# The end of the last down unit taken apart by product, and the second token tile back on the common load queue

## The chip, the cores and the metric

The kernel runs on one core of a Trainium2 chip. The metric is device microseconds of one execution. The times below are from four runs of the kernel before; one of them was profiled.

The engines are named as in the profile: PE (TensorE, matrix products; PEld its weight loads), DVE (VectorE), ACT (ScalarE), POOL (GpSimd), and SP, which here only issues DMA transfers. PE writes its products into PSUM, which has eight banks of 512 float32 columns per partition; DVE and ACT bring them from there to SBUF.

## The reference, cut to what matters

x is (1, 2048, 1024), all weights are bfloat16.

```python
xn = layernorm(x)
# linear attention, 32 heads of 32
q, k, v = split(xn @ wqkv)
pq, pk = phi(q), phi(k)                    # phi(t) = where(t > 0, t + 1, exp(t)) + 1e-6
kv = einsum("bhsd,bhse->bhde", pk, v); z = einsum("bhsd->bhd", pk)
s = (pq @ kv / (pq @ z + 1e-6)) @ wo
# feed-forward, F = 3584
g = silu((silu(xn @ w_gate) * (xn @ w_up)) @ w_down)
return x + s * g
```

## The kernel before, in words

The work is in stages that run one behind the other on PE.

**QKV stage** (to about 130 us). x is cut into 16 tiles of 128 tokens (`NT`), the K and V weights into four chunks of 512 columns (`NCH`, tile `wkv_sb`). Each token tile i is loaded (`load_x`), its statistics are taken by DVE (`emit_stats`, L409 and L410), the inverse deviation is made (for tiles 0 and 1 by ACT's square root, L422; from tile 2 by a Newton iteration, `emit_rstd`, on DVE for tile 2 and on POOL from tile 3), and it is normalised by DVE (`emit_N`, L447). PE needs it transposed. For tiles 0 to 3 (`NPE` = 4) PE transposes it itself (`emit_TR`, L474), and ACT or DVE copies the result out of PSUM (L479, L477); from tile 4 a transposing DMA on SP's queue does (L464). Then come four products per tile, `emit_Bmm(i, c)` (L490), eight matmuls each into one of three PSUM banks `kv_ps`. `emit_Bev(i, c)` empties a bank: for K by ACT (L144 and L151) and DVE (L152 and L153), for V by an ACT copy (L505). `emit_C(i)` (L512) accumulates K times V over all tiles.

The order on PE, DVE, ACT and POOL is that of the calls, written out by hand for the first tiles (a `manual_schedule`); each engine runs its instructions in that order and waits where its operands or its buffer are not ready. SP's queue is in the order of the calls too. The loads of x, of the K and V weights and then of the Q and output weights (12 MB in all) stand on it one behind the other, and the transposing DMAs of tiles 4 and up stand behind them. In the kernel before, three transfers go another way or have a special place: half of tile 0 and all of tile 1 are issued by ACT (L354, L357), and tile 1 is treated in halves like tile 0. PE's order in the first part is: products (0,0); transposes of 1; (0,1), (1,0), (1,1), (0,2); transposes of 2; (1,2), (2,0), (0,3), (1,3); C(0); transposes of 3; C(1); (2,1) and on.

**Attention stage** (to about 230 us), then **the feed-forward** in two passes of 1024 tokens. Its gate and up products (L731) and its down product (L916) are done by a scheme with seven products of half-size blocks in place of eight, whose sums are put together on DVE.

**The down product** (`emit_down`). A unit t (four per pass) is 128 tokens in each half of a pass, and has four output blocks of 128 by 512. Phase "a" makes one of them, and partial sums that three others need; for units 0 and 1 these are kept in SBUF (`kept`: s1 for one block, s34 for two). Phase "b" then adds three more products of 14 matmuls each (`prods_b`): two go to the two halves of a two-bank tile `dzw`, one to a bank `dx`. For units 0 and 1 the products are fresh in PSUM and DVE adds the kept partials on evacuation (`evac_b`, L975 and L976), ACT applies Silu with a scale (L977, L978), and `fin` multiplies by s and adds x on DVE (L888, L889) and stores the block (L890, on SP's queue in the last pass).

The very last unit, t = 1 of the last pass, is made by `finish`. PE runs the two products of `dzw` one after the other, then that of `dx`. DVE adds the kept partials to both halves of `dzw` in one instruction of 1024 columns (L1000), ACT applies Silu to both in one (L1001), and both blocks go through `fin`. For `dx`, DVE adds the kept partial in two instructions of 256 columns (L1008), each followed by ACT's Silu (L1009), and `fin` runs on each half of 256 columns with a store of its own.

The PSUM pools of this stage are `pps` (four tiles of one bank, tag "s") and `ppd` (two tiles of two banks, tag "d").

Of the kernel before, what the change touches and what calls it, by code (L numbers as in the profile page):

```python
# [9 lines left out]
ACT = mybir.ActivationFunctionType  # L10
ALU = mybir.AluOpType
FP32 = mybir.dt.float32
BF16 = mybir.dt.bfloat16
I32 = mybir.dt.int32
F32R = mybir.dt.float32r
F16 = mybir.dt.float16
# [5 lines left out]
def kernel(  # L22
# [11 lines left out]
    nc = tc.nc  # L34
    P = 128
    x2 = A_x.flatten_outer_dims()
# [295 lines left out]
    with ExitStack() as p1:  # L332
# [12 lines left out]
        def x_ap(i):  # L345
            return xp_tiles[i // 4][:, i % 4, :]
# [3 lines left out]
        def load_x(i):  # L350
            if i == 0 and D % 2 == 0:
                h = D // 2
                x_loads[i] = nc.sync.dma_start(out=x_ap(i)[:, 0:h], in_=x2[0:P, 0:h])
                nc.scalar.dma_start(out=x_ap(i)[:, h:D], in_=x2[0:P, h:D])  # L354
                return
            if i == 1:
                x_loads[i] = nc.scalar.dma_start(out=x_ap(i), in_=x2[i * P:(i + 1) * P, :])  # L357
                return
            x_loads[i] = nc.sync.dma_start(out=x_ap(i), in_=x2[i * P:(i + 1) * P, :])

        def load_wkv(c, halves=1):
            hs = DC // halves
            return [nc.sync.dma_start(out=wkv_sb[:, h * hs:(h + 1) * hs, c * CW:(c + 1) * CW],
                                      in_=wqkv_v[:, h * hs:(h + 1) * hs, D + c * CW: D + (c + 1) * CW])
                    for h in range(halves)]
# [1 line left out]
        NCH = 2 * NCC  # L367
        first_wave = min(2 * TPB, NT)
        load_x(0)
        load_x(1)  # L370
        load_wkv(0, halves=2 if DC % 2 == 0 else 1)
        nx = 2
        for c in range(1, NCH):
            load_wkv(c)
            if nx < NT:
                load_x(nx)
                nx += 1
        for i in range(nx, NT):
            load_x(i)
        for wt, wv in ((wq_sb, wqkv_v), (wo_sb, wo_v)):  # L380
# [71 lines left out]
        def emit_N(i):  # L452
            xn = xnw.tile([P, D], BF16, name="xn", tag="xn")
            xn_tiles[i] = xn
            if i < 2:
                for hh in range(2):
                    cols = slice(hh * (D // 2), (hh + 1) * (D // 2))
                    emit_norm(i, xn[:, cols], cols=cols)
            else:
                emit_norm(i, xn[:])  # L460
            ln_state.pop(i)
            if i >= NPE:
                xn_tiles.pop(i)
                nc.sync.dma_start_transpose(out=xn_ap(slice(0, DC), slice(i * P, (i + 1) * P)), in_=xn[:])  # L464

        def emit_TR(i):
            tok = slice(i * P, (i + 1) * P)
            xn = xn_tiles.pop(i)
            nh = 2 if i < 2 else 1
            dch = DC // nh  # L470
            for hh in range(nh):
                tr_ps = psC.tile([P, dch, P], BF16, name="tr_ps", tag="C")
                for dc in range(dch):
                    nc.tensor.transpose(tr_ps[:, dc, :], xn[:, (hh * dch + dc) * P:(hh * dch + dc + 1) * P], ident[:])  # L474
                dst = xn_ap(slice(hh * dch, (hh + 1) * dch), tok)
                if i == 1 and hh == 0:
                    nc.vector.tensor_copy(out=dst, in_=tr_ps[:])  # L477
                else:
                    nc.scalar.copy(out=dst, in_=tr_ps[:])  # L479
# [5 lines left out]
        def emit_Bmm(i, c):  # L485
            tok = slice(i * P, (i + 1) * P)
            kv_ps = psB.tile([P, CW], FP32, name="kv_ps", tag="B")
            kv_banks[(i, c)] = kv_ps
            for dc in range(DC):
                mm = nc.tensor.matmul(kv_ps[:], lhsT=xn_ap(dc, tok), rhs=wkv_sb[:, dc, c * CW:(c + 1) * CW],  # L490
                                      start=(dc == 0), stop=(dc == DC - 1))
                if dc == 0 and c == 0:
                    marks[("B", i)] = mm
# [49 lines left out]
        emit_Bev(1, 0)  # L543
        emit_Bmm(1, 1)
        emit_Bmm(0, 2)
        emit_TR(2)
        emit_Bev(1, 1)
        emit_Bev(0, 2)
        emit_Bmm(1, 2)
        emit_Bev(1, 2)  # L550
        emit_N(3)
        ln_pre(4)
        emit_Bmm(2, 0)
        emit_Bmm(0, 3)
        emit_Bev(0, 3)
        emit_Bmm(1, 3)
# [1 line left out]
        emit_C(0)  # L558
        for i in range(2, NT):
            for c in range(NCH):  # L560
                if (i, c) != (2, 0):
                    emit_Bmm(i, c)
                if c == 0:
                    if i + 1 < NPE:
                        emit_TR(i + 1)
                    emit_C(i - 1)
                emit_Bev(i, c)
                if c == 3 and i in (4, 6, 7):
                    prep(1)
                if i >= 8 and c % 2 == 1:  # L570
                    k = 2 * (i - 8) + c // 2
                    prep(11 * (k + 1) // 16 - 11 * k // 16)
                if c % 2 == 1:
                    for k in (PRE_AT[i - 1] if i - 1 in PRE_AT else (4,) if i == 2 else ())[c // 2:c // 2 + 1]:
                        emit_N(k)
                    for k in PRE_AT.get(i, ())[c // 2:c // 2 + 1]:
                        ln_pre(k)
# [140 lines left out]
    with ExitStack() as p3:  # L718
# [7 lines left out]
        def k2(shape, dt, name):  # L726
            return kp.tile(shape, dt, name=name, tag="k2")
# [156 lines left out]
        def fin(p, t, cc, y, eng1, eng2, out_eng, cols=None):  # L884
            io = io_tiles[(p, t, cc)]
            r0 = p * TB2 + t * P
            cs = cols or slice(0, CW)
            eng1.tensor_tensor(out=y[:, cs], in0=y[:, cs], in1=io[:, 1, cs], op=ALU.mult)  # L888
            eng2.tensor_tensor(out=io[:, 0, cs], in0=y[:, cs], in1=io[:, 0, cs], op=ALU.add)  # L889
            out_eng.dma_start(out=out2[r0:r0 + P, cc * CW + cs.start:cc * CW + cs.stop], in_=io[:, 0, cs])  # L890
            if cs.stop == CW:
                io_load()

        def emit_down(p, h, base, last, more_S, next_S):
# [5 lines left out]
            def wb(k, q):  # L900
                t = w_tiles[(p, "b", k // 2)]
                v = t[:].rearrange("p h a b -> p (h a b)")[:, 0:6 * CW].rearrange(
                    "p (k q n) -> p k q n", k=2, q=3)[:, k % 2, q]
                return v.bitcast(F16) if q == 2 else v
# [4 lines left out]
            def alloc(t, phase):  # L909
                x_ = pps.tile([P, CW], FP32, name="dx", tag="s")  # L910
                y_ = pps.tile([P, CW], FP32, name="dy", tag="s") if phase == "a" else None
                zw = ppd.tile([P, 2, CW], FP32, name="dzw", tag="d")
                bk[t] = (x_, y_, zw)

            def mm(out, lhs, rhs, first, lastk):
                nc.tensor.matmul(out, lhsT=lhs, rhs=rhs, start=first, stop=lastk, skip_group_check=True)  # L916
# [12 lines left out]
            def prods_b(t, k, fresh):  # L929
                x_, y_, zw = bk[t]  # L930
                f, l = fresh and k == 0, k == NFG - 1
                t2 = slice(TB + t * P, TB + (t + 1) * P)
                return [lambda: mm(x_[:], h[:, 2 * k + 1, t * P:(t + 1) * P], wb(k, 0), f, l),
                        lambda: mm(zw[:, 0, :], h[:, 2 * k + 1, t2], wb(k, 2), f, l),
                        lambda: mm(zw[:, 1, :], h[:, 2 * k, t2].bitcast(F16), wb(k, 1), f, l)]
# [51 lines left out]
                        lambda: fin(p, t, 0, g11, *fin_e)]  # L987

            def finish(t):
                alloc(t, "b")  # L990
                x_, _, zw = bk[t]
                s1, s34 = kept[t]
                for q in (1, 2):
                    for k in range(NFG):
                        prods_b(t, k, True)[q]()
                d = m4.tile([P, 2, CW], FP32, name="dd", tag="m4")
                c11 = k2([P, CW], FP32, "c11")[:]
                g_ = k2([P, 2, CW], BF16, "g12")
                g11 = k2([P, CW], BF16, "g11")[:]
                nc.vector.tensor_tensor(out=d[:], in0=zw[:], in1=s34, op=ALU.add)  # L1000
                nc.scalar.activation(out=g_[:], in_=d[:], func=ACT.Silu, scale=rch)  # L1001
                fin(p, t + TPB, 0, g_[:, 0, :], *fin_e)
                fin(p, t, 1, g_[:, 1, :], *fin_e)
                for k in range(NFG):
                    prods_b(t, k, True)[0]()
                hs_ = [slice(i * CW // 2, (i + 1) * CW // 2) for i in range(2)]
                for cs in hs_:
                    nc.vector.tensor_tensor(out=c11[:, cs], in0=x_[:, cs], in1=s1[:, cs], op=ALU.add)  # L1008
                    nc.scalar.activation(out=g11[:, cs], in_=c11[:, cs], func=ACT.Silu, scale=rch)  # L1009
                for cs in hs_:  # L1010
                    fin(p, t, 0, g11, *fin_e, cols=cs)

            NS = NFG + LEAD
# [209 lines left out]
```

## Time and profile before

| | us |
|---|---|
| median of 4 runs | 766.25 |
| the four runs | 765.86, 765.88, 766.63, 767.33 |
| the profiled run | 765.88 |
| its span | 764.0 |
| outside the span | 1.88 |
| mean granted TensorE clock | 0.999 |

The span is the time from the first to the last event of the core's profile; the time of a run has 1.88 us more in it. Rows of the timeline read: start, duration (both us from the span's start), engine, line of the kernel, operation, output tile and input tiles, shapes, count; in brackets the idle time of that engine just before, and what ended it. A group of several matmuls is shown as one row; a single 512-column matmul is listed with 379 ns, but they overlap, and start 216 ns apart (14 of them stretch over 3.19 us, that is 13 x 0.216 + 0.379). "PEq", "SPq" and the like are the sequencers that issue.

### The profile page before, as it was taken

To read this page: it belongs to the slowest core of one execution; us is meant where nothing else is said; L and a number is where in the kernel's file an instruction comes from. 1 tells how busy PE (TensorE), PEld (TensorE's weight loads), DVE (VectorE), ACT (ScalarE), POOL (GpSimd) and SP (SyncE) were. 2 spreads that over 40 slices of the span, in tenths; PEclk is the share of its full clock that TensorE was granted. 3 is DMA by queue.
4 is the path that set the end of the run, shared out by engine and by line. 5 is a ranking of instruction groups with operands and counts; after the bars stand their busy time and mean duration, and the time that the engine had idled before them with its cause. 6 is when DMAs were issued, how large, how long until landed. Compare 5 with 4: busy or idle time off the path is not lost.

```text
span 764.0 us, 10416 instructions
## 1 busy us (share of the span) xinstructions
PE 748.6 (98%) x3648; PEld 349.2 (46%) x3717; DVE 551.1 (72%) x1075; ACT 347.2 (45%) x476; POOL 287.7 (38%) x413
## 2 busy tenths in 40 slices
PE   8999999999999999999999999999999999999996
PEld 3444444444444444444444444444444444444443
DVE  7788567997666688888889875368676776787335
ACT  4535666788953566566448311132322223201111
POOL 0577599959674256868655000100000000200000
PEclk9999999999999999999999999999999999999999
DMA  9956867669789669898888136498644455520923
GB/s 316 350 102 122 213 247 250 268 214 279 229 292 272 247 233 314 299 345 299 298 301 301 65 104 246 126 379 313 231 171 166 166 173 180 189 105 28 296 70 118
DMA packets 105396, 170.29 MB, mean 223 GB/s; under 512 B 34688, under 2 KB 82176, under 8 KB 94720
## 3 DMA queue, kind: packets, MB, share of 16 engines
q1 hardware_dynamic: 94816, 120.74, 50.3%
q0 software_dynamic: 7936, 44.31, 14.8%
q10 hardware_dynamic: 2592, 4.59, 1.8%
q8 instruction: 29, 0.48, 0.2%
q14 instruction: 23, 0.19, 0.1%
HBM read 111.67 MB, written 50.59 MB: 212 GB/s over the span
## 4 chain that ended last, share of the span: by engine, by line
PE 88%; DVE 6%; DMA 2%; issue 1%; POOL 1%; ACT 1%; SPq 0%; DVEq 0%; ACTq 0%
PE zw L731 25%; PE xb L731 12%; PE dzw L916 12%; PE kv_ps L490 11%; PE s_ps L665 7%; PE yb L731 6%; PE dx L916 6%; PE q_ps L170 4%; PE dy L916 3%; DMA xp<-in_A_x_dram 1%; DMA xnT<-xn 1%; PE kvz L512 1%; DVE o_blk L646 1%; PE nd_ps L638 1%; DVE pqT L141 1%
## 5 line engine op out<-in xcount | busy, mean ns | idle before, releaser
L731 PEld LDWEIGHTS <-w_sb 128*128 128x128 f16 (+1 forms) x1568 | 152.2, 98 | 182.8
L490 PE MATMUL kv_ps<-wkv_sb,xnT 128*128 128x512 bf16 x499 | 113.0, 379 | 3.1 <-DMA wkv_sb<-in_A_wqkv_dram 0.9
L731 PE MATMUL xb<-xnT,w_sb 128*128 128x512 bf16 x420 | 113.3, 379 | 1.5
L731 PE MATMUL zw<-S,w_sb 128*128 128x512 f16 x448 | 105.8, 379 | 0.0
L731 PE MATMUL zw<-xnT,w_sb 128*128 128x512 bf16 x448 | 105.8, 379 | 0.0
L280 POOL TENSOR_TENSOR w_sb<-w_sb 128x512 f16<-128x512 bf16 x42 | 48.9, 1165 | 95.6 <-DVE w_sb L268 36.3
L247 ACT ACTIVATE w_sb<-w_sb 128x2048 bf16<-128x2048 bf16 x42 | 79.9, 1902 | 6.1 <-DMA w_sb<-in_B_w_up_dram 5.3
L916 PE MATMUL dx<-w_sb,hT 128*128 128x512 bf16 x216 | 79.7, 379 | 0.3
L490 PEld LDWEIGHTS <-xnT 128*128 128x128 bf16 x512 | 48.6, 97 | 58.6 <-issue 1.6
L916 PEld LDWEIGHTS <-hT 128*128 128x128 bf16 (+1 forms) x448 | 43.8, 98 | 52.8
L916 PE MATMUL dzw<-w_sb,hT 128*128 128x512 bf16 (+1 forms) x217 | 63.0, 379 | 0.1
L170 PE MATMUL q_ps<-xnT,wq_sb 128*128 128x512 bf16 x249 | 57.9, 379 | 0.4
L665 PE MATMUL s_ps<-wo_sb,oT 128*128 128x512 bf16 x250 | 57.4, 379 | 0.3
L731 PE MATMUL yb<-S,w_sb 128*128 128x512 f16 x224 | 57.4, 378 | 0.0
L759 DVE SCALAR_TENSOR_TENSOR s<-yb,rc_all,s 128x512 f32<-128x512 f32 x42 | 31.5, 749 | 35.4 <-ACT s L758 35.2
L807 ACT ACTIVATE sg<-cg 128x1024 bf16<-128x1024 f32 x28 | 29.6, 1057 | 57.6 <-DVE cg L800 57.5
L800 DVE SCALAR_TENSOR_TENSOR cg<-zw,rc_all,s 128x1024 f32<-128x1024 f32 x28 | 35.9, 1283 | 25.4 <-PE zw L731 14.0
L856 POOL TENSOR_TENSOR hs<-hT 128x512 f16<-128x512 bf16 x2 | 2.5, 1254 | 132.6 <-ACT sg L807 132.6
L281 POOL TENSOR_TENSOR w_sb<-w_sb 128x512 f16<-128x512 bf16 x42 | 50.1, 1193 | 3.3
L283 POOL TENSOR_TENSOR w_sb<-w_sb 128x512 f16<-128x512 bf16 x42 | 50.8, 1210 | 0.0
L282 POOL TENSOR_TENSOR w_sb<-w_sb 128x512 f16<-128x512 bf16 x42 | 49.8, 1186 | 0.0
L890 POOL DMA_DIRECT2D out_dram<-io x16 | 8.7, 542 | 101.9 <-DVE io L889 101.6
(148 smaller groups left out, 1100.9 us busy)
## 6 DMA issues: line engine op xcount, KB each, us to landing
w_sb<-pk_g SPq DMA_DIRECT2D x27, 1024.0 KB, 5.7
pk_g<-w_sb POOLq DMA_DIRECT2D x14, 1024.0 KB, 5.1
pk_u<-w_sb POOLq DMA_DIRECT2D x14, 1024.0 KB, 5.8
w_sb<-wd SPq DMA_DIRECT2D x14, 1024.0 KB, 5.2
w_sb<-pk_u SPq DMA_DIRECT2D x14, 1024.0 KB, 5.0
w_sb<-wd SPq DMA_DIRECT2D x14, 768.0 KB, 4.5
w_sb<-in_B_w_gate_dram SPq DMA_DIRECT2D x14, 512.0 KB, 4.9
w_sb<-in_B_w_down_dram SPq DMA_DIRECT2D x28, 256.0 KB, 3.4
```

The costliest lines, as they stand in the source:

```text
L170: nc.tensor.matmul(q_ps[:], lhsT=wq_sb[:, dc, g * P:(g + 1) * P], rhs=xn_ap(dc, btok), start=(dc == 0), stop=(dc == DC - 1))
L247: nc.scalar.activation(out=junk, in_=raw_view(key, t), func=ACT.Square, accum_out=asum[:])
L280: nc.gpsimd.tensor_tensor(out=T1, in0=b12, in1=b11, op=ALU.subtract)
L281: nc.gpsimd.tensor_tensor(out=T2, in0=b22, in1=T1, op=ALU.subtract)
L282: nc.gpsimd.tensor_tensor(out=T3, in0=b22, in1=b12, op=ALU.subtract)
L283: nc.gpsimd.tensor_tensor(out=T4, in0=b21, in1=T2, op=ALU.subtract)
L490: mm = nc.tensor.matmul(kv_ps[:], lhsT=xn_ap(dc, tok), rhs=wkv_sb[:, dc, c * CW:(c + 1) * CW], start=(dc == 0), stop=(dc == DC - 1))
L665: mm = nc.tensor.matmul(s_ps[:], lhsT=oT[:, c, ttok], rhs=wo_sb[:, c, cc * CW:(cc + 1) * CW], start=(c == 0), stop=(c == G - 1))
L731: mm = nc.tensor.matmul(out, lhsT=lhs(k), rhs=rhs(k), start=(first and k == 0), stop=(k == HK - 1), skip_group_check=True)
L759: nc.vector.scalar_tensor_tensor(out=s2[:], in0=y_[:], scalar=rc, in1=s1[:], op0=ALU.mult, op1=ALU.add)
L800: nc.vector.scalar_tensor_tensor(out=d12, in0=zw[:], scalar=rc, in1=s2[:, None, :].to_broadcast([P, 2, TB]), op0=ALU.mult, op1=ALU.add)
L916: nc.tensor.matmul(out, lhsT=lhs, rhs=rhs, start=first, stop=lastk, skip_group_check=True)
```

## The change

Two places are changed.

In the QKV stage, tile 1 is no longer issued on ACT's queue: it goes on SP's queue, after the two halves of the first weight chunk and ahead of the second chunk. It is normalised in one instruction and transposed in one group of eight, and DVE in place of ACT copies the transposes of tiles 0 and 1 out of PSUM. The transposes of tile 2 and its first product (2,0) move back: PE's order becomes (0,0); transposes of 1; (0,1), (1,0), (1,1), (0,2), (1,2); transposes of 2; (0,3), (1,3); C(0); (2,0); transposes of 3; C(1); (2,1) and on.

In `finish`, each product gets a PSUM bank of its own: product 0 half of a two-bank tile (`dz`), product 1 a bank `df0`, and the last product two banks `df1` and `df2`, 256 columns in each. Products 0 and 1 each have their own addition and Silu of 512 columns. The kept partial of the last block is copied by ACT into `df1` and `df2` ahead of the products, and PE accumulates on it (`first` is False for all matmuls of that product), so that no addition follows. The last product runs in two column halves one after the other, 14 matmuls of 256 columns each, with its weights loaded for each half; Silu reads each half from PSUM.

```diff
@@ load_x @@
-            if i == 1:
-                x_loads[i] = nc.scalar.dma_start(out=x_ap(i), in_=x2[i * P:(i + 1) * P, :])
-                return
             x_loads[i] = nc.sync.dma_start(out=x_ap(i), in_=x2[i * P:(i + 1) * P, :])
...
         load_x(0)
-        load_x(1)
         load_wkv(0, halves=2 if DC % 2 == 0 else 1)
-        nx = 2
+        nx = 1
         for c in range(1, NCH):
-            load_wkv(c)
             if nx < NT:
                 load_x(nx)
                 nx += 1
+            load_wkv(c)
@@ emit_N @@
-            if i < 2:
+            if i == 0:
@@ emit_TR @@
-            nh = 2 if i < 2 else 1
+            nh = 2 if i == 0 else 1
...
-                if i == 1 and hh == 0:
+                if i < 2:
                     nc.vector.tensor_copy(out=dst, in_=tr_ps[:])
                 else:
                     nc.scalar.copy(out=dst, in_=tr_ps[:])
@@ order of the first tiles @@
         emit_Bmm(0, 2)
-        emit_TR(2)
         emit_Bev(1, 1)
...
         ln_pre(4)
-        emit_Bmm(2, 0)
+        emit_TR(2)
         emit_Bmm(0, 3)
...
         for i in range(2, NT):
             for c in range(NCH):
-                if (i, c) != (2, 0):
-                    emit_Bmm(i, c)
+                emit_Bmm(i, c)
@@ finish(t) @@
-                alloc(t, "b")
-                x_, _, zw = bk[t]
+                ps = [ppd.tile([P, 2, CW], FP32, name="dz", tag="d")[:, 0, :]]
+                ps += [pps.tile([P, CW], FP32, name="df%d" % i, tag="s")[:] for i in range(3)]
                 s1, s34 = kept[t]
-                for q in (1, 2):
+                t1, t2 = slice(t * P, (t + 1) * P), slice(TB + t * P, TB + (t + 1) * P)
+                hs_ = [slice(i * CW // 2, (i + 1) * CW // 2) for i in range(2)]
+                for i in range(2):
+                    nc.scalar.copy(out=ps[2 + i][:, 0:CW // 2], in_=s1[:, hs_[i]])
+                for q, (r0, cc) in enumerate(((t + TPB, 0), (t, 1))):
                     for k in range(NFG):
-                        prods_b(t, k, True)[q]()
-                d = m4.tile([P, 2, CW], FP32, name="dd", tag="m4")
-                c11 = k2([P, CW], FP32, "c11")[:]
-                g_ = k2([P, 2, CW], BF16, "g12")
+                        lhs = h[:, 2 * k, t2].bitcast(F16) if q else h[:, 2 * k + 1, t2]
+                        mm(ps[q], lhs, wb(k, 2 - q), k == 0, k == NFG - 1)
+                    d = k2([P, CW], FP32, "d%d" % q)[:]
+                    g_ = k2([P, CW], BF16, "g%d" % q)[:]
+                    nc.vector.tensor_tensor(out=d, in0=ps[q], in1=s34[:, q, :], op=ALU.add)
+                    nc.scalar.activation(out=g_, in_=d, func=ACT.Silu, scale=rch)
+                    if q == 0:
+                        f0 = (r0, cc, g_)
+                fin(p, *f0, *fin_e)
+                fin(p, r0, cc, g_, *fin_e)
                 g11 = k2([P, CW], BF16, "g11")[:]
-                nc.vector.tensor_tensor(out=d[:], in0=zw[:], in1=s34, op=ALU.add)
-                nc.scalar.activation(out=g_[:], in_=d[:], func=ACT.Silu, scale=rch)
-                fin(p, t + TPB, 0, g_[:, 0, :], *fin_e)
-                fin(p, t, 1, g_[:, 1, :], *fin_e)
-                for k in range(NFG):
-                    prods_b(t, k, True)[0]()
-                hs_ = [slice(i * CW // 2, (i + 1) * CW // 2) for i in range(2)]
-                for cs in hs_:
-                    nc.vector.tensor_tensor(out=c11[:, cs], in0=x_[:, cs], in1=s1[:, cs], op=ALU.add)
-                    nc.scalar.activation(out=g11[:, cs], in_=c11[:, cs], func=ACT.Silu, scale=rch)
-                for cs in hs_:
+                for i, cs in enumerate(hs_):
+                    o_ = ps[2 + i][:, 0:CW // 2]
+                    for k in range(NFG):
+                        mm(o_, h[:, 2 * k + 1, t1], wb(k, 0)[:, cs], False, k == NFG - 1)
+                    nc.scalar.activation(out=g11[:, cs], in_=o_, func=ACT.Silu, scale=rch)
                     fin(p, t, 0, g11, *fin_e, cols=cs)
```

## The prediction, on record before the changed kernel ran

> **What bounds the kernel now.** I read the page first, then the chain of work that ended last, then the timeline of the two places that the change touches: the first 45 us and the last 16 us.
>
> ```profile
> span 764.0 us, 10416 instructions
> PE 748.6 (98%) x3648; PEld 349.2 (46%) x3717; DVE 551.1 (72%) x1075; ACT 347.2 (45%) x476; POOL 287.7 (38%) x413
> PE 88%; DVE 6%; DMA 2%; issue 1%; POOL 1%; ACT 1%; SPq 0%; DVEq 0%; ACTq 0%
> ```
>
> TensorE (PE) is busy 98% and carries 88% of the chain. So the change can move the time only where PE waits or where the span runs on after PE's last matmul. Such places are few: the start, and the tail behind PE's last product.
>
> The run that was profiled took 765.88 us for its span of 764.0, so 1.88 us lie around the span. The median of the four runs is 766.25, 0.37 above that run. I work out a difference in the span and take it from the median.
>
> **The tail, before.** This is the timeline of the last 10 us: start, duration, engine, line, operation, and what ended the idle time.
>
> ```profile
> 754.88 3.19 PE L916 MATMUL dx<-w_sb,hT 128*128 128x512 bf16 x14
> 755.08 1.23 DVE L1000 TENSOR_TENSOR dd<-dzw,kept 128x1024 f32<-128x1024 f32 x1 [1.05 <-PE dzw L916]
> 756.34 1.15 ACT L1001 ACTIVATE g<-dd,hsc 128x1024 bf16<-128x1024 f32 x1 [4.29 <-DVE dd L1000]
> 757.52 0.43 DVE L888 TENSOR_TENSOR g<-g,io 128x512 bf16<-128x512 bf16 x1 [1.21 <-ACT g L1001]
> ...
> 758.78 0.42 DVE L889 TENSOR_TENSOR io<-g,io 128x512 bf16<-128x512 bf16 x1
> 759.12 0.75 DVE L1008 TENSOR_TENSOR c<-dx,kept 128x256 f32<-128x256 f32 x2
> 759.57 0.91 ACT L1009 ACTIVATE g<-c,hsc 128x256 bf16<-128x256 f32 x2 [2.08 <-DVE c L1008]
> 760.12 0.29 DVE L888 TENSOR_TENSOR g<-g,io 128x256 bf16<-128x256 bf16 x1 [0.24 <-ACT g L1009]
> ...
> 760.97 0.29 DVE L889 TENSOR_TENSOR io<-g,io 128x256 bf16<-128x256 bf16 x1
> ```
>
> PE ends at 758.07 (754.88 + 3.19), but VectorE (DVE) only takes up PE's last result at 759.12: it is still busy with the two products before, whose joint 1024-wide addition could not start until both were done (755.08). Its last addition ends at 761.26, 3.19 us after PE. What follows (the last store's issue, landing, the end) takes 2.74 us to 764.0 and is not touched.
>
> **The tail, after.** Product 0 now ends by itself, 14 matmuls earlier. The 28 matmuls before 755.05 are spaced 0.216, so product 0 is done at 755.05 - 14 x 0.216 = 752.03. DVE is then still writing out the unit before (its last L889, at 753.60 for 0.42, ends 754.02). The 512-wide addition takes 0.68 (L976, same shapes): 754.05 to 754.73. The Silu takes 0.70 (L978): to 755.46. Product 1 is done at 755.05: addition 755.08 to 755.76, Silu 755.79 to 756.49. Four multiplications and additions of L888 and L889 stretch over 1.60 (757.52 to 759.12 above) and start at 755.79: they end at 757.40, while PE is still at work.
>
> The last product becomes 28 matmuls of 256 columns, with 14 more weight loads. No row has 256 columns. The nearest are 512 columns, spaced 0.216, and 129 columns with a fresh weight load each (L512), eight in 0.46 on the chain, so 0.058 each. In a straight line between them 256 columns cost 0.110. So 28 take 3.05 instead of 14 x 0.216 = 3.02, and PE ends near 758.10. Bounds: no less than half of 0.216 (3.02 in all), no more than a full 0.216 each (6.05, +3.0 us). I take 0.110: the 129-column row shows pairs of load and matmul at half that spacing, so the load is hidden.
>
> A weight load reads 97 to 98 ns as busy on the page. The Trainium skill ("TensorE: Matmul & The Clock Gate", the section on LDWEIGHTS) gives columns / 1.2 ns for it, 107 ns for 128 columns; if loads could overlap nothing, 14 more would cost an estimated 1.5 us by that page and the time would be 765.8. The L512 row, a load and a matmul every 0.058, speaks against that.
>
> The kept partial no longer has to be added by DVE after PE: two ScalarE (ACT) copies of 256 columns put it into the banks ahead. The 512-wide copy L955 takes 0.585, so each takes at most that. They stand on ACT behind L978, free at 752.05, and are done by 753.2; PE's first matmul of the last product waits for them and comes at 754.88: cover of 1.6 us. Behind them on ACT stands product 0's Silu, not ready before 754.73. Copying into the accumulator bank appears in no row; twice the time would still be covered.
>
> The end is then a short chain. PE's second half ends at 758.10; Silu from PSUM, 256 wide, 0.50 (L1009; L983 and L978 take 0.69 and 0.70 from PSUM and from SBUF, so the source does not matter): 758.13 to 758.63. Then L888 and L889 as at 760.65 to 761.26, 0.61: 758.68 to 759.29. The first half is done by 758.0 beside PE. **Gain: 761.26 - 759.29 = 1.97 us.** SP's store queue has no work between 758.4 and 759.3, so the last store goes at once.
>
> **The start.** Token tile 1 loses its own queue (ACT) and goes on SP behind both halves of the first weight chunk; its normalisation loses its halves; DVE instead of ACT evacuates the transposes of tiles 0 and 1; tile 2's transposes and its first product go back to later places. These are rows of the timeline:
>
> ```profile
> 8.89 0.65 PE L474 MATMUL tr_ps<-ident,xn 128*128 128x128 bf16 x8
> ...
> 10.43 7.07 PE L490 MATMUL kv_ps<-wkv_sb,xnT 128*128 128x512 bf16 x31 [0.89 <-DMA wkv_sb<-in_A_wqkv_dram]
> ...
> 11.10 1.29 DVE L409 BATCH_NORM_STATS2 stats<-xp 128x6 f32<-128x512 bf16 x2 [1.36 <-DMA xp<-in_A_x_dram]
> ```
>
> Before, tile 1 landed at 1.20 + 4.4 = 5.6. The later half of the weight chunk landed near 7.4 (issued at 1.67; the two halves took 5.2 in the median, the faster 4.7, so the slower 5.7). Behind it tile 1 lands near 7.4, since the sum of bytes is the same. Statistics of tile 1 start at 7.45, not 6.26 (DVE's two new copies, 0.42 each, end at 7.34). Normalisation starts 2.09 later as before, 9.54, takes 0.54 in one piece, and the eight transposes start at 10.18 and let PE go on at 10.65. Before, PE went on at 10.43 because of the second weight chunk, whose place in the bytes is unchanged: +0.22.
>
> DVE then copies tile 1's transposes (two times 0.42), so tile 2's statistics start at 11.67, not 11.10: the DVE chain is 0.57 late, and with it ScalarE's L144 and L151 for the product (1,0), ended by L153 at 16.56, now 17.13. They free its bank at 18.34. Product (1,2) takes that bank, and PE is ready for it at 10.65 + 32 x 0.216 = 17.56, since tile 2's transposes no longer stand ahead of it. PE idles 0.8. The old wait of 0.32 at 20.03 and the 0.17 that the transposes took longer there go. Added up, PE reaches the product (2,1), where the orders agree again, at 27.1 instead of 26.57: **0.55 late**.
>
> That lateness meets a wait. First the chain, then the timeline:
>
> ```profile
> 31.73 0.55 DVE xn L447
> 32.30 7.81 DMA xnT<-xn
> 40.16 1.25 PE kv_ps L490 x5
> ```
>
> ```profile
> 40.16 1.90 PE L490 MATMUL kv_ps<-wkv_sb,xnT 128*128 128x512 bf16 x7 [0.88 <-DMA xnT<-xn]
> ```
>
> PE waits 0.88 for tile 4's transposing DMA. That was issued at 32.30, yet the DMA view shows the engines full (about 350 GB/s) to past 37, on the weight loads ahead of it in the same queue; later transposes land in 3.1. So the landing at 40.1 is set by the end of the loads, and issuing it 0.57 later changes nothing (some 4 us of slack). PE arrives at 39.28 + 0.55 = 39.83, still too early. **The start costs 0.** If that cover goes, it costs what is left over: lateness minus 0.88. Below nothing: at most 0.3 is to be had, if the loads drain sooner. Above: see B and D.
>
> **Sum.** 764.0 - 1.97 = 762.0 for the span, 763.9 for a run like the profiled one; 766.25 - 1.97 = **764.3** for the median, 0.26% less. What a measurement of this kernel can tell from no change is about 0.2%, 1.53 us, so faster means below 764.7 and slower above 767.8.
>
> **Rivals.**
>
> A, the forecast (0.61): 763.4 to 764.8 with the scatter of the runs.
>
> B, the start outlasts its cover (0.17): between the first product's end (7.0 + 8 x 0.216 = 8.7) and 10.18 PE now idles 1.5 us, where it idled 0.89. The warm-up matmuls of 512 columns (eleven at 0.43 in 1.49 to 5.88) show that PE starts at half rate. If the longer idle time brought that back for as long, the loss is some 3.6 / 2 = 1.8: 0.55 + 1.8 - 0.88 = 1.5, giving 765.8. A DVE or ACT chain 0.6 later than I reckon gives 764.6 to 765. Against it: 0.89 idle at 9.54 left the next 32 matmuls at 0.216.
>
> By the Trainium skill (the same page, "The HAM clock gate") the clock falls only after an idle window of about 3.4 us, which would make the first of these nothing; no row here has such a gap after the warm-up.
>
> C, weight loads show in the 256-column matmuls (0.12 in all): each 0.01 us above 0.110 costs 0.27. At 0.14 to 0.18 the time is 765.1 to 766.2 (0.08). The gain is gone at 0.110 + 1.97 / 27 = 0.183, and beyond it the kernel is **slower**: at the bound of 0.216 the end is 3.0 later, 764.3 + 3.0 = 767.3 (0.04, of which 0.03 by over 0.2% only with B added). Against: the L512 row.
>
> D, the transposing DMA lands elsewhere (0.10): 256 KB move from one DMA queue to another, 0.73 us at 350 GB/s; either sign. Earlier: 764.0. Later: up to 765.0.
>
> That the change does not do what it says would be a Silu on the first half that waits for the second; the halves have separate banks and each Silu its own wait on PE, so I give this nothing of its own.
>
> **Chances.** Faster by over 0.2%: A 0.60, and 0.05 of D and 0.01 of B: 0.66. Slower by over 0.2%: 0.03, from C with B. Within: 0.31. Range: from 763.4 (A with D's gain) to 766.0 (B and most of C), leaving out C's far end.
>
> **What would show it.** Tail: the last DVE row ends 1.2 us behind PE's last matmul instead of 3.2; 28 matmuls of 256 columns in about 3.2; no DVE addition behind PE. Start: PE waits once near 17.6 to 18.4 for ACT, comes to the wait at 40.1 with 0.3 left of 0.88, and all is level from there to 748. The prediction is wrong if PE's last product begins later than 754.9, or if its spacing exceeds 0.12.

## The result, and the profile after

Over 40 runs the changed kernel takes 765.31 us in the median (763.63 to 767.86), the kernel before, over 61 runs, 766.58 (lowest 765.6). The ratio is **0.9979 (95% interval 0.9970 to 0.9987)**: 0.21% faster, where 0.26% was forecast. Ratios here compare undisturbed runs alone, so they are not quite the quotients of the medians.

The run that was profiled took 767.84 us, the second slowest of all, and its span is longer than that of before, though the kernel is faster. So this profile is to be read place by place, not as a whole. Its page:

```profile
span 766.1 us, 10444 instructions
...
PE 92%; DVE 4%; ACT 1%; issue 1%; DMA 1%; SPq 0%; ACTq 0%; DVEq 0%
```

PE's share of the chain (the work that ended last, followed back) is 92% instead of 88: PE carries the start as well now, behind tile 1's load (2.21 to 8.92 in the chain), and DVE has less of the tail.

The tail, from the timeline of the last 13 us (a group's row shows the shape of its first matmul only; 28 of these are 256 wide):

```profile
755.89 6.24 PE L910 MATMUL df<-w_sb,hT 128*128 128x512 bf16 x41
...
756.00 0.66 ACT L990 COPY df<-kept 128x256 f32<-128x256 f32 x2
...
759.17 0.68 DVE L997 TENSOR_TENSOR d<-df,kept 128x512 f32<-128x512 f32 x1
...
760.64 0.47 ACT L1008 ACTIVATE g<-df,hsc 128x256 bf16<-128x256 f32 x1
...
762.17 0.47 ACT L1008 ACTIVATE g<-df,hsc 128x256 bf16<-128x256 f32 x1 [1.05 <-PE df L910]
762.68 0.29 DVE L882 TENSOR_TENSOR g<-g,io 128x256 bf16<-128x256 bf16 x1 [0.37 <-ACT g L1008]
763.00 0.29 DVE L883 TENSOR_TENSOR io<-g,io 128x256 bf16<-128x256 bf16 x1
```

PE ends at 762.13 and DVE's last row at 763.29, 1.16 us behind it; before it was 3.19. The end gained 2.03 us, and no DVE addition stands behind PE.

The start, from the timeline of the first 48 us:

```profile
8.94 1.29 DVE L405 BATCH_NORM_STATS2 stats<-xp 128x6 f32<-128x512 bf16 x2 [1.65 <-DMA xp<-in_A_x_dram]
...
11.63 0.62 PE L470 MATMUL tr_ps<-ident,xn 128*128 128x128 bf16 x8 [2.64 <-DVE xn L443]
...
29.41 7.07 PE L486 MATMUL kv_ps<-wkv_sb,xnT 128*128 128x512 bf16 x31
...
36.77 7.07 PE L486 MATMUL kv_ps<-wkv_sb,xnT 128*128 128x512 bf16 x32
```

Tile 1 lands at 8.9, not 7.4. PE idles 2.64 us ahead of its transposes and reaches (2,1) at 29.41 instead of 26.57. Right behind that idle time, the table of stretches shows another thing (columns: the stretch and its length, busy time and instructions of PE, PEld, DVE, ACT and POOL, then PEclk, the granted clock, which is the share of its full rate that PE is given, DMA share, GB/s):

```profile
11.00:12.70 1.70, 1.07 (x11) 0.76 (x12) 0.96 (x2) 1.69 (x3) 0.00 (x0) 1.00 1.09 352
12.80:16.20 3.40, 3.40 (x10) 1.21 (x9) 3.02 (x14) 1.48 (x3) 0.00 (x0) 0.50 1.09 356
16.30:18.00 1.70, 1.65 (x8) 0.78 (x8) 1.49 (x8) 0.00 (x0) 0.00 (x0) 1.00 1.08 368
```

From 12.8 to 16.2 the granted clock is 0.50, and PE is busy throughout with ten matmuls in the stretch, those at its edges counted; at 0.216 apart it would be some seventeen.

The waits of PE have two more that were not there before, near 340 us in the first feed-forward pass:

```profile
PE tr_ps L470 <- DVE xn L443: 2.6, 1, 2.6
PE warm_ps L521 <- DVE warm L518: 1.5, 1, 1.5
PE yb L251 <- DVE s L753: 1.0, 1, 1.0
...
PE zw L725 <- DVE cg L794: 0.9, 1, 0.9
```

In this run, then: end -2.03; start +1.79 (product (4,0) begins at 36.77 + 24 x 0.216 = 41.95 instead of 40.16); the waits near 340 us +2.2, together +2.0 of the +2.1. The two waits are 1.0 and 0.9 of idle time and 0.16 more each: a matmul is listed with 0.379, but without the wait the next would have started 0.216 after it. Which of the last two belong to the change, and how often they come, is what the experiments ask.

### The profile page after: what moved, and what is told of

Read it like the earlier page. It is cut to its first block, busy times and chain, and to the rows that moved or that the text cites. A ratio compares the mean times of both kernels' runs of the same rounds, so it can differ in the third digit from the quotient of the medians.

```text
span 766.1 us, 10444 instructions
## 1 busy us (share of the span) xinstructions
PE 750.6 (98%) x3662; PEld 351.0 (46%) x3731; DVE 551.1 (72%) x1075; ACT 346.4 (45%) x476; POOL 287.3 (38%) x413
## 4 chain that ended last, share of the span: by engine, by line
PE 92%; DVE 4%; ACT 1%; issue 1%; DMA 1%; SPq 0%; ACTq 0%; DVEq 0%
PE zw L725 25%; PE kv_ps L486 14%; PE xb L725 12%; PE dzw L910 12%; PE s_ps L659 7%; PE yb L725 6%; PE dx L910 6%; PE q_ps L170 4%; PE dy L910 3%; PE kvz L508 1%; DMA xp<-in_A_x_dram 1%; PE df L910 1%; DVE o_blk L640 1%; PE nd_ps L632 1%; DVE pqT L141 1%
## 5 line engine op out<-in xcount | busy, mean ns | idle before, releaser
L486 PE MATMUL kv_ps<-wkv_sb,xnT 128*128 128x512 bf16 x499 | 114.6, 383 | 0.8 <-DVE xnT L473 0.2
L910 PE MATMUL dx<-w_sb,hT 128*128 128x512 bf16 x202 | 76.6, 379 | 0.3
L910 PE MATMUL dzw<-w_sb,hT 128*128 128x512 f16 (+1 forms) x190 | 57.0, 379 | 0.0
```

## The experiments

Each was timed beside the kernel before on the same chip; the chips differ between groups, so ratios are better compared than medians. All but one have the new end or a part of it.

| | median us | of before | ratio (95%) |
|---|---|---|---|
| new end, old start | 764.57 | 766.13 | 0.9973 (0.9963 to 0.9983) |
| old end, new start | 767.09 | 766.13 | 1.0016 (0.9998 to 1.0033) |
| changed, tile 1 on its own queue | 763.97 | 766.13 | 0.9968 (0.9954 to 0.9982) |
| the same again | 764.01 | 765.97 | 0.9972 (0.9963 to 0.9980) |
| changed, idle time filled | 764.43 | 766.13 | 0.9972 (0.9961 to 0.9983) |
| changed again | 764.50 | 765.89 | 0.9983 (0.9972 to 0.9995) |
| end: own banks only | 764.85 | 765.89 | 0.9988 (0.9979 to 0.9996) |
| end: banks and copied partial | 764.91 | 765.89 | 0.9984 (0.9974 to 0.9994) |
| changed, tile 1 later still | 769.08 | 765.97 | 1.0040 (1.0027 to 1.0053) |
| the same, idle time filled | 767.32 | 765.97 | 1.0014 (1.0005 to 1.0023) |

**The two halves of the change by themselves.** First the kernel before with the `finish` of the changed one.

> The start of before with the new end. Theory T (the end gives its full 1.97 us, and what the changed kernel lacks of that it loses at the start): 764.5 against 766.5 of before, ratio 0.9974, and the last DVE row ends about 1.2 us behind PE's last matmul. Rival E (the end itself gives less than its rows say, since something behind it waits, and the start costs nothing): the same ratio as the whole change, 0.9979.

Measured: 0.9973, 1.56 us less in the median, the lowest run 763.66 against 765.49 (-1.83). In its profile PE ends at 753.07 + 6.24 = 759.31 and DVE at 760.47, 1.16 behind. The ratio alone does not part 0.9974 (theory T) from 0.9979 (rival E), since its interval takes in both; the rows do, for they show the full gain. Then the changed kernel with the old `finish`.

> The new start with the end of before. Theory T: slower than before by what the whole change lacks of 1.97 us, 0.3 to 0.9 us in the median (ratio 1.0004 to 1.0012), in single runs between 0 and 2, as the runs of the changed kernel scatter between 763.6 and 767.9; tile 1 lands at 7.4 to 8.9 us and PE idles 1.5 to 2.6 ahead of its transposes. Rival E: level with before within 0.2 us, and PE comes to tile 4's transposing DMA with some of the 0.88 us of waiting left.

Measured: 1.0016, with an interval that takes in no change; 0.96 us more in the median, the lowest run 0.26 above the lowest of before. In its profile tile 1's statistics start at 8.67, PE idles 2.16, keeps the full rate, reaches (2,1) at 28.07 and is held by tile 4's DMA for only 0.18 us, starting (4,0) at 40.80. For the end theory T holds. For the start, 0.96 stands against 0.3 to 0.9 expected, with an interval that takes in no change: that the start alone loses is likely, not certain, by this pair; the next ones make it firmer.

**Tile 1 on its own queue**, all else as changed:

```diff
+            if i == 1:
+                x_loads[i] = nc.scalar.dma_start(out=x_ap(i), in_=x2[i * P:(i + 1) * P, :])
+                return
...
         load_x(0)
+        load_x(1)
         load_wkv(0, halves=2 if DC % 2 == 0 else 1)
-        nx = 1
+        nx = 2
         for c in range(1, NCH):
+            load_wkv(c)
             if nx < NT:
                 load_x(nx)
                 nx += 1
-            load_wkv(c)
```

> The changed kernel, with tile 1 alone put back on ACT's queue ahead of the first weight chunk; order, halves and copies stay as changed. Theory Q (the start loses because tile 1 lands late): tile 1 lands near 5.6, its statistics start at 7.4, its transposes near 10.1, PE idles 1.4 and keeps the full rate, and the time is that of the new end with the old start, 764.4 (ratio 0.9974). Theory O (it is the order of PE and the copies on DVE that lose): no better than the changed kernel, 0.9979.

Measured: 0.9968, and 0.9972 on another chip:

> The changed kernel with tile 1 alone on ACT's queue, once more, as the candidate for the fastest version: 764.0 to 764.5, ratio 0.997 to 0.998, if the first figure (0.9968) holds. In its profile PE waits for tile 4's transposing DMA at about 40 us, so that the start costs nothing.

In the first of the two profiles the rows of the start come out as the prediction had meant for the changed kernel itself:

```profile
7.32 1.28 DVE L409 BATCH_NORM_STATS2 stats<-xp 128x6 f32<-128x512 bf16 x2
...
10.00 0.62 PE L474 MATMUL tr_ps<-ident,xn 128*128 128x128 bf16 x8 [0.97 <-DVE xn L447]
...
27.04 7.07 PE L490 MATMUL kv_ps<-wkv_sb,xnT 128*128 128x512 bf16 x31
...
40.23 1.90 PE L490 MATMUL kv_ps<-wkv_sb,xnT 128*128 128x512 bf16 x8 [0.49 <-DMA xnT<-xn]
```

PE is 0.47 late at (2,1) (27.04 against 26.57) and still waits 0.49 for tile 4's DMA; in the other profile it is 0.78 late and waits 0.19. Both are near the spread of the old start itself, which reaches (2,1) between 26.39 and 27.24 in its five profiles, and begin (4,0) at 40.23 and 40.24, within the old start's 39.98 to 40.39. So the new order, the transposes in one piece and the copies on DVE cost nothing that this wait does not take up: by the rows theory O falls. What costs is when tile 1 lands.

The first of these profiles is of the slowest of its twelve runs (768.02), for a reason elsewhere: PE idles 0.88 and 1.15 us near 334, and the granted clock is then 0.50 from 335.87 to 339.28. Half rate behind idle time is not a matter of the start alone.

**The idle time filled.** Ten matmuls that nothing reads keep PE busy behind the first product:

```diff
         emit_Bmm(0, 0)
+        fps = psC.tile([P, CW], FP32, name="fill_ps", tag="C")
+        for k in range(10):
+            nc.tensor.matmul(fps[:], lhsT=warm[:, 0:P], rhs=warm[:], start=True, stop=True)
         emit_TR(1)
```

> The changed kernel with ten matmuls of 512 columns on a zeroed tile into a bank that nothing reads, put between the first product and the transposes of tile 1, where PE was idle for 2.6 us in the profiled run and then ran ten matmuls at 0.43 us instead of 0.216. They add 2.2 us of PE work. Theory G (the idle time brings back half rate): the matmuls behind the transposes start 0.216 apart, the product (2,1) starts 1 to 2 us earlier than 29.4, and the time is 0.5 to 1 us below the changed kernel. Theory L (late data alone costs): the rate of those matmuls or the start of (2,1) does not improve, and the time is level with the changed kernel or above it.

Measured: 0.9972, seven runs within 763.82 to 764.85. No half-rate stretch in the profile, (2,1) at 27.62. But in this profile tile 1 landed at 7.6, so the idle time without the filling would have been shorter too, and (4,0) begins at 40.16 as in the kernel before; this run does not settle which of the two helped. The next pair does: tile 1 goes behind the second weight chunk, without filling and with 22 such matmuls.

```diff
         for c in range(1, NCH):
+            if c == 1:
+                load_wkv(c)
             if nx < NT:
                 load_x(nx)
                 nx += 1
-            load_wkv(c)
+            if c > 1:
+                load_wkv(c)
```

> The changed kernel with tile 1 a further place back on SP's queue, behind the second weight chunk: it lands near 11 us, its transposes start near 14, and PE idles some 5 us behind its first product. Theory G (a long idle time brings half rate back for a stretch of 3.41 us, as the clock record of the changed kernel's two profiles shows at 12.79 and at 11.47): the record shows such a stretch in this profile too, 1.7 us are lost by it, and (2,1) starts near 31.5; with 0.88 covered, the time is 3 to 4 us above the new end alone. Theory L: no such stretch; the first matmuls behind the transposes start 0.216 apart, and (2,1) starts near 29.8.

> The same, with 22 matmuls of 512 columns on a zeroed tile in the idle stretch (4.7 us of PE work that nothing reads). Theory G: no half-rate stretch behind them, (2,1) starts 1.5 us or more earlier than without them, and the time is lower by as much. Theory L: (2,1) starts at the same time as without them.

Tile 1's statistics start at 11.88 and 11.95, and its transposes at 14.58 and 14.65: the same lateness in both. The stretch behind it, first without, then with filling:

```profile
12.80:19.50 6.70, 4.92 (x18) 2.30 (x19) 4.79 (x17) 3.11 (x5) 0.00 (x0) 0.50 1.09 363
```

```profile
12.80:19.50 6.70, 6.09 (x34) 2.89 (x34) 5.14 (x19) 3.75 (x6) 0.00 (x0) 1.00 1.09 362
```

Without filling the clock is 0.50 for 6.83 us (12.77 to 19.60 in the clock record, two of the stretches that theory G expected one of), and PE gets 18 matmuls done where it gets 34 with it. (2,1) starts at 33.11 against 31.34, and the medians are 769.08 against 767.32: 1.77 and 1.76 us. Without filling the median stands some 4.5 us above that of the new end with the old start (769.08 against 764.57, on another chip), where 3 to 4 was expected with one such stretch; with filling some 2.8. Theory G holds: it is idle time on PE that brings back the half rate, and useless work that prevents it makes the kernel faster.

**Both kernels once more.** The changed one unaltered:

> The changed kernel once more, beside the next two, for a second look at its start and at the wait near 340 us. Theory S (two things scatter: when tile 1 lands, and a load of the up weights near 340 us that comes late in some runs of every kernel): the median lies 0.5 to 1 us above that of the kernel with the new end alone, ratio about 0.998, and in this profile one or both of the waits differ from the first one, where they cost 1.96 and 1.9 us. Rival W (the wait near 340 us belongs to the changed kernel): it is there again with 1 us or more.

Measured: 0.9983. In its profile tile 1's statistics start at 8.72, PE idles 2.33, the half rate lasts from 11.47 to 14.88, (2,1) starts at 29.18, and (4,0) at 36.54 + 24 x 0.216 = 41.72: a start of +1.56. One of the two waits near 340 us is there (0.9).

> The kernel before once more, one look. Theory S: a time between 765.5 and 768, and if it is over 767, PE waits 1 to 2 us near 340 us for ACT or DVE behind a late load of the up weights, as in the changed kernel's first profile. Rival W: no such wait, whatever the time.

A single run of the kernel before: this time 768.24, with a start like that of its first profile ((2,1) at 26.39, 0.89 left at tile 4's DMA). PE's waits:

```profile
PE xb L731 <- ACT sg L806: 1.2, 1, 1.2
PE yb L251 <- DVE s L759: 1.1, 1, 1.1
```

And the waits on DMA between 235 and 420 us:

```profile
ACT w_sb L247 <- DMA w_sb<-in_B_w_up_dram: 9.5, 4, 6.8
```

A load of up weights comes late (up to 6.8 us of waiting on ACT, where the first profile of before has 2.3), ACT and DVE fall behind, and PE waits 2.2 us (1.05 and 1.15). Of the twelve profiles other than the first of before, eight show such a wait of PE, 0.4 to 2.2 us, whatever they change. Rival W falls: the +1.9 us near 340 is not the change's. Why that load is late in some runs was not looked into.

**The end in parts**, on the old start. First own banks, additions and Silus alone: the last product stays whole, and DVE adds behind it:

```diff
                 c11 = k2([P, CW], FP32, "c11")[:]
...
                 for k in range(NFG):
...
+                    mm(ps[2], h[:, 2 * k + 1, t1], wb(k, 0), k == 0, k == NFG - 1)
                 for cs in hs_:
-                    nc.vector.tensor_tensor(out=c11[:, cs], in0=x_[:, cs], in1=s1[:, cs], op=ALU.add)
+                    nc.vector.tensor_tensor(out=c11[:, cs], in0=ps[2][:, cs], in1=s1[:, cs], op=ALU.add)
                     nc.scalar.activation(out=g11[:, cs], in_=c11[:, cs], func=ACT.Silu, scale=rch)
```

> The start of before; of the new end only the own bank, addition and Silu for each product; the last product stays one of 512 columns, and DVE adds the kept partial behind it in two halves. Worked out from the rows: PE ends at 758.07, the additions run 758.10 to 758.89, Silus to 759.43, the last four DVE rows to 760.1, so 1.2 of the 1.97 us are gained: ratio 0.9985, the last DVE row 2.0 us behind PE. Rival H (the halves and the copied partial are what counts): less than 0.6 us, 0.9992.

Then with the partial copied into the bank (`nc.scalar.copy(out=ps[2], in_=s1)`, matmuls with `first` False) and Silu in halves from PSUM, the product still whole:

> The start of before; the new end with the partial copied into the bank, but the last product in one piece of 512 columns, with Silu in two halves behind it. Worked out: PE ends at 758.07, the Silus run 758.10 to 759.01 (starts 0.41 apart, 0.50 each), DVE from 758.65 to 759.66: 1.6 of 1.97 us, ratio 0.9979, the last DVE row 1.6 us behind PE. If the 256-column pieces cost PE time, this is the fastest end of the three.

From the two timelines, in this order:

```profile
758.81 0.75 DVE L1012 TENSOR_TENSOR c<-df,kept 128x256 f32<-128x256 f32 x2 [0.59 <-PE df L916]
...
760.73 0.29 DVE L889 TENSOR_TENSOR io<-g,io 128x256 bf16<-128x256 bf16 x1
```

```profile
759.48 0.84 ACT L1012 ACTIVATE g<-df,hsc 128x256 bf16<-128x256 f32 x2 [1.52 <-PE df L916]
...
760.84 0.29 DVE L889 TENSOR_TENSOR io<-g,io 128x256 bf16<-128x256 bf16 x1
```

| end | PE's end | last DVE row | behind PE | gained |
|---|---|---|---|---|
| before | 758.07 | 761.26 | 3.19 | |
| own banks | 752.57 + 6.21 = 758.78 | 761.02 | 2.24 | 0.95 |
| and copied partial | 753.23 + 6.21 = 759.44 | 761.13 | 1.69 | 1.50 |
| and column halves (new end) | 759.31 | 760.47 | 1.16 | 2.03 |

So, added in this order, the own banks give 0.95 of the 2.03 (1.2 was expected), the copied partial 0.55 (0.4) and the halves 0.53. The lowest runs point the same way: 764.59, 764.05 and (on the other chip) 763.66. The medians of the first two do not tell the parts from each other (764.85 and 764.91), with the scatter near 340 us in them.

## Why the prediction was right, and which step failed

The number came out: 0.21% (0.13 to 0.30) where 0.26% was forecast, and the mechanism of the tail is the one that was reckoned. The step that failed is the start: it was put at 0 on the ground that tile 1 lands near 7.4, and it cost 1.79 and 1.56 us in the two profiles of the changed kernel. That the median stayed so near the forecast is in part luck, since this loss is not the same in every run.

- **The tail: right.** 1.97 us were reckoned, 2.03 measured. The 28 matmuls of 256 columns are 0.109 apart (the last two products of 6.24, less 14 x 0.216 and the last one's own 0.27, over 27), where 0.110 was taken between the rows of 129 and 512 columns (28 of these come to 3.08, not 3.05; a slip of 0.03); 14 more weight loads cost nothing, and rival C is out. The copies take 0.36 each, under the bound of 0.585, and Silu from PSUM 0.47 instead of 0.50. The cover beside PE is thinner than reckoned: DVE waits 0.57 for a load (`io<-s_dram`) until 757.76, its rows for the first two products end 0.34 ahead of PE's end instead of 0.70, and those of the first half 0.18 behind it. DVE still idles 0.37 before the last two rows, so nothing is lost.
- **"Behind it tile 1 lands near 7.4, since the sum of bytes is the same": wrong.** Its statistics start at 8.94, 8.72 and 8.67 in three profiles and at 7.63 in one. The bytes were indeed moved by then (1 MB is 1024 x 1024 bytes here): the packets that had ended by 7.4 us hold 1.75 MB in the changed kernel and 1.78 in the one before, more than the 1.5 MB of tile 0, the first chunk and tile 1. But 2.26 MB had been moved when tile 1 was complete at 8.91: part of what stood behind it on the queue was done before it. Why, no run here shows.
- **"The start costs 0": right only where the lateness stays under the cover.** The cover is 1.04, not 0.88: without the wait (4,0) would have begun 0.216 after the matmul before it, at 33.94 + 24 x 0.216 = 39.12, not at that one's listed end. With tile 1 on its own queue the lateness is 0.47 and 0.78, as reckoned (0.55), and the cover holds. With tile 1 landing at 8.6 to 8.9 on SP's queue it is 1.5 at the full rate and 2.6 to 2.8 with the half-rate stretch.
- **Rival B came true in part.** Its mechanism, half rate after idle time, was there in both profiles of the changed kernel, and the start cost 1.79 and 1.56 us there against the 1.5 reckoned; the half rate was absent in the profile with the old end. The idle time was 2.64 and 2.33 us, not 1.5, since tile 1 came later. In the median the start takes back an estimated 0.5 to 1.1 us: 0.9979 and 0.9983 stand against 0.9968 to 0.9973 with tile 1 on its own queue or the old start. The intervals overlap, and that of 0.9979 takes in the forecast, so this size is less certain than the rows.
- **The page and the traces.** By the Trainium skill ("TensorE: Matmul & The Clock Gate", "The HAM clock gate") it takes an idle window of about 3.4 us for the clock to fall. Here 2.64 and 2.33 us of idle time were followed by it, and 2.16 in another profile was not. The measurement decides; the length of the half-rate stretches, 3.41 and 6.83 us, is one and two of that page's windows.
- **When the clock falls.** In all thirteen profiles the granted clock falls only at whole multiples of 3.41 us after its first rise (5.96 and 12.79 in the changed kernel's first profile, 4.64 and 11.47 in its second). The stretch of 3.41 us just before a fall held between 0 and 1.53 us of PE work (1.16 and 1.08 in these two, 1.53 before the fall at 335.87); no such stretch with 1.67 us or more was followed by one. The 2.16 us of idle time that did no harm lay across a mark of this grid at 10.24, with 2.16 and 2.29 us of work on its two sides. So here it is where idle time lies on the grid that decides, not its length alone, and since the first rise comes between 4.64 and 6.83, the same idle time can cost in one run and not in another. This is read from the traces; no run was made to test it.
- **Rival D was seen, but cost little.** Where tile 1 came at 8.6 to 8.9, tile 4's transpose landed at 40.76, 41.07 and 41.19 (39.63 to 40.34 in the profiles where tile 1 was there by 7.6), and PE was later than that in two of the three; in the profile with the old end it was held for 0.18 us.
- **A sign that misled.** "The prediction is wrong if PE's last product begins later than 754.9": that did come, for it begins at 752.87 + 28 x 0.216 = 758.92 in the changed kernel, and at 753.07 + 14 x 0.216 = 756.09 with the old start. The shift is the start (1.8) and the waits near 340 us (2.2), not the tail, and of the waits the prediction had nothing ("all is level from there to 748"). The distance from PE's end to DVE's last row tests the tail; the time at which the last product begins does not.

The fastest version found is the changed kernel with tile 1 alone on ACT's queue: 763.97 and 764.01, ratios 0.9968 and 0.9972. The old start with the new end, 0.9973, is not to be told from it.

## What to carry to other kernels

Behind the last matmul, count the chain of instructions from PE to the last store: give each product its own bank and evacuation, let PE do the last addition by accumulating on a partial that was put into the bank ahead, and cut the last product into columns so that only a small piece is left behind it. A transfer that PE soon needs is not dated by the bytes ahead of it on its queue; if it must be early, it wants a queue without large transfers. The copied partial worked in banks that full-width matmuls had written before; no run here tries it in others. And idle time may cost more than its length, since PE can run at half rate after it: look at the granted clock of that stretch, not at its mean over the span.

## What the runs showed of the hardware that was not expected

- A granted clock of 0.50 for 3.41 us after 2.3 to 2.6 us of idle time on PE, or after 0.88 and 1.15 us close together, and for 6.83 us after 5.3 us; after 2.16 us it stayed at 1.00. With 22 unread matmuls in the longest of these gaps it stayed at 1.00.
- A transfer of 256 KB, behind two of 512 KB on the same queue and ahead of one of 1 MB, was complete only when 2.26 MB had been moved, some 0.7 MB more than what stood up to it.
- Loads of up weights near 340 us landed so late in most profiles that PE waited 0.4 to 2.2 us, in the kernel before too; a difference of 2 us between two single runs of this kernel says nothing.
